# First layer of a retention + two-MLP kernel: seven half products for eight in groups 1 to 3, and everything behind the retention put in order by a list scheduler in the source

## The chip, the cores and the metric

The kernel runs on one core of one Trainium2 chip. The metric is device time of one execution in microseconds (us), as the median of three runs. Engines are named as the profile names them: PE is TensorE (its weight loads are PEld), DVE is VectorE, ACT is ScalarE, POOL is GpSimd, SP is the engine that issues most DMAs.

## What is computed

The reference has three parts, one behind the other: a retention (a decayed running sum of outer products of k and v, read with q) over 2 batches, 8 heads, 768 positions and 64 channels; a first layer pair with a softplus; and a second, gated layer pair behind a norm.

```python
for t in range(S):
    state = gamma[None, :, None, None] * state + np.einsum('bhd,bhe->bhde', k[:, :, t], v[:, :, t])
    y[:, :, t] = scale * np.einsum('bhd,bhde->bhe', q[:, :, t], state)
x = y.transpose(0, 2, 1, 3).reshape(1536, 512)
h = x @ w_in                                   # 512 -> 2048
x = (np.maximum(h, 0.0) + np.log1p(np.exp(-np.abs(h)))) @ w_out      # 2048 -> 512
xn = x / np.sqrt(np.mean(x * x, axis=-1, keepdims=True) + 1e-06) * rms_g
g = xn @ w_gate                                # 512 -> 1536
out = (g * (1.0 / (1.0 + np.exp(-g))) * (xn @ w_val)) @ w_out2       # 1536 -> 512
```

The weights arrive as 64-bit floats and are turned into 32-bit floats on the chip.

## The kernel before

Tokens (1536) lie along the free dimension in three blocks of 512: block 0, block 1 and block 2, which the code calls `LONE`. Channels lie on the 128 partitions. A product of float32 precision is made of three matmuls (`TERMS`): every operand is kept as a rounded high part and the remainder, its low part, and high by high, high by low and low by high are summed in one PSUM bank. The unit of PE work is a matmul of 128 x 128 weights by 128 x 512 tokens.

**Weights.** Each of the 68 weight tiles is loaded as 64-bit words (`st_...`), and its float32 value is put together by `convert`: two ACT passes (`c`, `a`), a shift and a bit operation on DVE (`w`), an integer add on POOL (`c<-w,c`, L206), a DVE pass (`a<-a,c`, L275), the high part on ACT (L224) and the low part (`rounded`, L221) on POOL, or on DVE for w_gate and w_val. Twelve buffers hold finished weights.

**First layer.** w_in has 16 tiles of 128 output channels, in 4 groups of 4. `l1(b, f)` makes the 12 matmuls (`h`) of one tile for one block; the softplus behind it is three ACT passes and one DVE pass that reads PSUM, then a split into high (ACT) and low (DVE). `l2(b, gr, m)` makes 12 matmuls of the product with w_out for a group. The two alternate, `l1` of one block with `l2` of the block before it. The sum over groups of blocks 0 and 1 is kept in SBUF by DVE adds (L601), that of block 2 in PSUM.

**Second layer.** Blocks 0 and 1 and pairs of weight tiles already go through class `Seven`: with x split into two blocks and two halves of the channels, and the weights likewise, seven half products of 6 matmuls each (`p1` to `p7`, banks Q, R, W) take the place of eight. They need sums of weight tiles (`S`, on POOL, L244), sums of token tiles (`T1` to `T4`), three copies out of bank Q (`c1`, `c6`, `c7`, by ACT) that must be done before the next product is added into Q, and adds of the results on DVE. Block 2 goes the plain way (`l3`). `l4` makes the product with w_out2 and adds over pairs.

**Order.** Program order on each engine is the order in which the source emits instructions. Before, that is written by hand: `piece` emits one PE step, then conversions, delayed work from `later(us, do)` against a hand-advanced `clock`, and one step of the chains that do the norm (`mean`, `along`, `scaled`) and the T sums. PE takes its instructions in that order and waits where an operand isn't ready.

Of the kernel before, what the change touches and what calls it, by code (L numbers as in the profile page):

```python
# [20 lines left out]
G1 = 4  # L21
TINY = 1.125 * 2.0 ** -15


@with_exitstack
def retention_softplus_swiglu(ctx: ExitStack, tc: tile.TileContext, q, k, v, w_in, w_out,
# [34 lines left out]
    oldest, kept = list(range(8)), []  # L61
# [5 lines left out]

    def lend():
        oldest.extend(kept)
        kept.clear()  # L70
# [22 lines left out]
    dec = const.tile([P, 2, CPB, H], F32)  # L93
# [21 lines left out]
    causal = const.tile([P, P], F32)  # L115
# [3 lines left out]
    state = [const.tile([P, NP, D], F32, name=f"state{i}") for i in range(2)]  # L119
    faded = const.tile([P, NP, D], F32, name="faded")  # L120
# [18 lines left out]
    st_free, lent = [f"st{i}" for i in range(STAGE)], []  # L139
    lending = []  # L140
# [19 lines left out]
    clock, due, raw, reserved, busy_s = [0.0], [], {}, [0], []  # L160
    raw_used, raw_at, spare = [0] * 3, {}, []

    def later(us, do):
        due.append((clock[0] + us, do))

    def run(all=False):
        for one in list(due):
            if one in due and (all or one[0] <= clock[0]):
                due.remove(one)
                one[1]()  # L170

# [3 lines left out]
    def convert(parts=False):  # L175
# [5 lines left out]
        gated = nm in ("w_gate", "w_val")  # L181
        if len(free) - reserved[0] < 1 or raw_used[spins.get("a", 0)]:
            return False
# [3 lines left out]
        raw_at[key] = spins.get("a", 0)  # L187
# [22 lines left out]
        raw[key] = a  # L210
        if gated and f % 2:
            sums, sa = [], []
            hold = 0 if key == ("w_val", 1) else 2
            reserved[0] += hold

        def used(n):
            for one in (f - 1, f):
                raw_used[raw_at[nm, one]] += n

# [11 lines left out]
        def combine():  # L231
            if busy_s:
                later(1.36, combine)
                return
            busy_s.append(key)
            a0, a1 = raw[nm, f - 1], a
            sa.extend(row(f"s{n}", "s") for n in range(2))
            s1, s2 = (halves(sa[0], p) for p in range(2))
            s3, s4 = (halves(sa[1], p) for p in range(2))
            for out, x0, x1, op in ((s1, halves(a1, 0), halves(a1, 1), ALU.add),  # L240
                                    (s2, s1, halves(a0, 0), ALU.subtract),
                                    (s3, halves(a0, 0), halves(a1, 0), ALU.subtract),
                                    (s4, halves(a0, 1), s2, ALU.subtract)):
                nc.gpsimd.tensor_tensor(out=out, in0=x0, in1=x1, op=op)  # L244
            used(-1)

            def parts():
                places = free if hold else spare
                if len(places) < 2 or clock[0] - freed.get(places[1], 0.0) < 2.7:
                    later(1.36, parts)  # L250
                    return
                reserved[0] -= hold
                for n in range(2):
                    slot["S", nm, f // 2, n] = places.pop(0)
                    sums.append(rows(slot["S", nm, f // 2, n], f"ws_s{n}"))
                    ws["S", nm, f // 2, n] = sums[n]
                    high(sums[n], sa[n])

                def rest():
                    for n, out in enumerate(sums):  # L260
                        rounded(out, sa[n])
                        ready.add(("S", nm, f // 2, n))
                    busy_s.clear()
                later(1.4, rest)
            later(4.0, parts)

        def whole():
            for out, src in ((ws[nm, f - 1], raw[nm, f - 1]), (t, a)):
                rounded(out, src, nc.vector)
            ready.add((nm, f - 1))  # L270
            ready.add(key)
            used(-1)

        def finish():
            nc.vector.scalar_tensor_tensor(out=a, in0=a, scalar=TINY, in1=c.bitcast(F32),  # L275
                                           op0=ALU.is_ge, op1=ALU.mult)
            if not gated:
                if nm == "w_out2":
                    later(2.6, last)
                else:  # L280
                    deferred.append(last)
            else:
                later(2.6, high)
                if f % 2:
                    later(1.3, combine)
                    later(4.0, whole)

        if gated and f % 2:
            used(2)
        ws[key] = t  # L290
        left[key] = 2 if gated else NB
        pos["conv"] += 1

        def done():
            (lent if lending else st_free).append(tag)
            lending[:] = []
# [7 lines left out]
        if nm in ("w_in", "w_out"):  # L304
            deferred.append(finish)
        else:
            later(5.4, finish)
        return True

    def need(key):  # L310
        while key not in ready:
            if due:
                run(True)
            elif deferred:
                flush()
            else:
                assert convert(), key
# [6 lines left out]
    freed = {}  # L324

    def release(tag):
        freed[tag] = clock[0]
        free.append(tag)
# [170 lines left out]
    g_t, acc, tags = {}, {}, {}  # L499
    bg = []  # L500
    chains = []
# [14 lines left out]
    def split_later(key, t):  # L516
        def go():
            n = places.pop(key, None)
            if n is None:
                n = places["next"]  # L520
                places["next"] = (n + 1) % 8
            g = rows(f"g{n}", "g")
            split(g[:, 0], g[:, 1], t)
            g_t[key] = g
        deferred.append(go)
# [26 lines left out]
    def kept_row(b, m, src):  # L552
        tags[b, m] = spin("s2_", 10)
        acc[b, m] = row(tags[b, m], "x2")
        if m % 2 and b == 0:
            nc.vector.tensor_copy(acc[b, m], src)
        else:
            nc.scalar.activation(out=acc[b, m], in_=src, func=AF.Copy)

    def l2_by(b, f):  # L560
        for m in range(KC):
            if f == 0:
                acc[b, m] = bank("l2", kept)
            w = weight("w_out", f, m == KC - 1)
            for n, (i, j) in enumerate(TERMS):
                nc.tensor.matmul(acc[b, m], lhsT=w[:, i, m * P:(m + 1) * P], rhs=g_t[b, f][:, j, :],  # L566
                                 start=(n == 0 and f == 0), stop=(n == 2 and f == G1 - 1))
        g_t.pop((b, f))

        def after():  # L570
            if f == G1 - 1:
                for m in range(KC):
                    kept_row(b, m, acc[b, m])
                lend()
        return after

    def l2(b, gr, m):
        fs = range(gr * G1, (gr + 1) * G1)
        keep = b == NB - 1
        if keep:  # L580
            if gr == 0:
                acc[b, m] = bank("l2", kept)
            p = acc[b, m]
        else:
            p = bank("l2")
        for f in fs:
            w = weight("w_out", f, m == KC - 1)
            for n, (i, j) in enumerate(TERMS):
                nc.tensor.matmul(p, lhsT=w[:, i, m * P:(m + 1) * P], rhs=g_t[b, f][:, j, :],  # L589
                                 start=(n == 0 and f == (0 if keep else fs[0])),  # L590
                                 stop=(n == 2 and f == (F1 - 1 if keep else fs[-1])))
        if m == KC - 1:
            for f in fs:
                g_t.pop((b, f))

        def after():
            if not keep:
                if gr == 0:
                    kept_row(b, m, p)
                else:  # L600
                    nc.vector.tensor_tensor(out=acc[b, m], in0=p, in1=acc[b, m], op=ALU.add)  # L601
            if gr == NG1 - 1:
                norm(b, m)
        return after

    root = {}
    root_t = const.tile([P, NB, CB], F32, name="root_t")  # L610
    small = const.tile([P, 2, CB], F32, name="small")
    sqs, rooted = {}, set()

    def norm(b, m):
        if m == 0:
            root[b] = row(("r", "ms", "r")[b], "root")
            sqs[b] = [rows(f"g{2 + n}" if b == LONE else f"x{2 + 2 * b + n}", "sq", F32) for n in range(2)]
            if b == LONE:
                channels(("n", b), b)
        sq, r = sqs[b], root[b]  # L620

        def high():
            if b == LONE:
                nc.scalar.activation(out=x["n", b][0][m // 2][:, m % 2], in_=acc[b, m], func=AF.Copy, scale=rg[:, m:m + 1])
# [610 lines left out]
```

## Time and profile before

| what | value |
|---|---|
| timed runs | 605.24, 605.32, 605.75 us, median 605.32 us |
| profiled execution | span 603.5 us from its first to its last instruction; no other time is recorded of it |
| PE busy | 596.8 us, 99% of the span |
| DVE, ACT, POOL busy | 452.9, 353.7, 278.0 us (75%, 59%, 46%) |
| chain that ended last | 94% PE |
| instructions | PE 3232, DVE 655, ACT 613, POOL 228 |

The span is what the trace shows; the timed runs lie 1.8 us above it. Busy PE isn't PE at its best, since the ends of pipelined matmuls are modelled; distances between starts tell more than durations.

### The profile page before, as it was taken

To read this page: it belongs to the slowest core of one execution; us is meant where nothing else is said; L and a number is where in the kernel's file an instruction comes from. 1 tells how busy PE (TensorE), PEld (TensorE's weight loads), DVE (VectorE), ACT (ScalarE), POOL (GpSimd) and SP (SyncE) were. 2 spreads that over 40 slices of the span, in tenths; PEclk is the share of its full clock that TensorE was granted. 3 is DMA by queue.
4 is the path that set the end of the run, shared out by engine and by line. 5 is a ranking of instruction groups with operands and counts; after the bars stand their busy time and mean duration, and the time that the engine had idled before them with its cause. 6 is when DMAs were issued, how large, how long until landed. Compare 5 with 4: busy or idle time off the path is not lost.

```text
span 603.5 us, 8624 instructions
## 1 busy us (share of the span) xinstructions
PE 596.8 (99%) x3232; PEld 494.7 (82%) x3232; DVE 452.9 (75%) x655; ACT 353.7 (59%) x613; POOL 278.0 (46%) x228
## 2 busy tenths in 40 slices
PE   8999999999999999999999999999999999999997
PEld 7888888888888888878878888888888888888886
DVE  5788777577777875258788988699799699799545
ACT  3456678787778775287575667653563563554320
POOL 3544344554445442224021277485386387287111
PEclk9999999999999999999999999999999999999999
DMA  9999133233333331121000112322222221320014
GB/s 199 229 222 218 48 106 102 78 99 106 104 81 99 99 105 36 35 64 42 1 2 0 36 35 71 104 71 70 71 71 55 85 71 36 105 70 2 1 53 156
DMA packets 65562, 48.84 MB, mean 81 GB/s; under 512 B 39792, under 2 KB 60528, under 8 KB 65520
## 3 DMA queue, kind: packets, MB, share of 16 engines
q1 hardware_dynamic: 64320, 47.90, 28.3%
q8 instruction: 25, 0.41, 0.3%
q10 hardware_dynamic: 1200, 0.39, 0.3%
q14 instruction: 17, 0.14, 0.1%
HBM read 45.14 MB, written 3.15 MB: 80 GB/s over the span
## 4 chain that ended last, share of the span: by engine, by line
PE 94%; SPq 2%; DVE 1%; DMA 1%; ACT 1%; issue 0%; DVEq 0%
PE h L509 22%; PE l L589 20%; PE l L916 16%; PE Q L806 10%; PE h_w_val L509 5%; PE h_w_gate L509 5%; PE R L806 5%; PE y L469 2%; PE W L806 2%; PE l L566 2%; PE sc L417 2%; SPq L84 1%; PE pt L398 1%; DMA st_w_in<-in_moe_w_in_dram 1%; PE u L436 1%; DVE g L784 0%
## 5 line engine op out<-in xcount | busy, mean ns | idle before, releaser
L206 POOL TENSOR_TENSOR c<-w,c 128x512 uint32<-128x512 uint32 x68 | 90.9, 1337 | 122.4 <-DVE w L202 91.5
L509 PE MATMUL h<-x,ws_w_in 128*128 128x512 f32 x576 | 137.5, 390 | 0.0
L509 PEld LDWEIGHTS h<-x,ws_w_in 128*128 128x128 f32 x576 | 107.7, 188 | 23.1 <-issue 0.7
L589 PE MATMUL l<-g,ws_w_out 128*128 128x512 f32 x528 | 125.4, 390 | 0.0
L589 PEld LDWEIGHTS l<-g,ws_w_out 128*128 128x128 f32 x528 | 98.7, 188 | 20.9 <-DVE g L125 0.6
L916 PE MATMUL l<-ws_w_out,g 128*128 128x512 f32 x432 | 108.2, 389 | 0.0
L916 PEld LDWEIGHTS l<-ws_w_out,g 128*128 128x128 f32 x432 | 81.0, 188 | 17.1 <-DVE g L784 0.3
L547 DVE SCALAR_TENSOR_TENSOR t<-h,t 128x512 f32<-128x512 f32 x48 | 33.1, 690 | 61.1 <-ACT t L540 61.1
L221 POOL TENSOR_TENSOR ws_w_out<-a,ws_w_out 128x512 fp32r<-128x512 f32 x28 | 39.6, 1414 | 57.0 <-ACT ws_w_out L224 57.0
L812 ACT ACTIVATE p<-Q 128x512 f32<-128x512 f32 x36 | 21.4, 596 | 59.1 <-PE Q L806 59.1
L275 DVE SCALAR_TENSOR_TENSOR a<-a,c 128x512 f32<-128x512 f32 x68 | 50.3, 739 | 7.0 <-POOL c L206 7.0
L124 ACT ACTIVATE g<-t 128x512 fp32r<-128x512 f32 x48 | 30.2, 629 | 34.0 <-DVE t L547 34.0
L221 POOL TENSOR_TENSOR ws_s<-s,ws_s 128x512 fp32r<-128x512 f32 x24 | 37.9, 1597 | 25.9 <-ACT ws_s L224 25.9
L535 ACT ACTIVATE t<-h 128x512 f32<-128x512 f32 x48 | 28.6, 596 | 33.2 <-PE h L509 33.1
L784 DVE TENSOR_TENSOR g<-t,g 128x512 fp32r<-128x512 f32 x36 | 36.7, 1043 | 13.3 <-ACT g L783 13.3
L827 POOL TENSOR_TENSOR t<-t,e 128x512 f32<-128x512 f32 x18 | 26.6, 1477 | 34.6 <-DVE e L823 23.2
L125 DVE TENSOR_TENSOR g<-t,g 128x512 fp32r<-128x512 f32 x48 | 33.9, 707 | 8.9 <-ACT g L124 6.0
L946 DVE TENSOR_TENSOR o<-l,o 128x512 f32<-128x512 f32 x39 | 26.6, 684 | 18.0 <-PE l L916 17.9
L806 PE MATMUL Q<-T,ws_s 128*128 128x512 f32 x144 | 36.5, 391 | 0.1
L221 POOL TENSOR_TENSOR ws_w_in<-a,ws_w_in 128x512 fp32r<-128x512 f32 x16 | 22.4, 1397 | 29.3 <-ACT ws_w_in L224 27.9
L202 DVE SCALAR_TENSOR_TENSOR w<-st_w_out,w 128x512 uint32<-128x512 uint32 x28 | 34.0, 1215 | 1.0
L509 PE MATMUL h_w_val<-x,ws_w_val 128*128 128x512 f32 x144 | 34.7, 390 | 0.0
(132 smaller groups left out, 1035.5 us busy)
## 6 DMA issues: line engine op xcount, KB each, us to landing
st_w_out<-in_moe_w_out_dram SPq DMA_DIRECT2D x28, 512.0 KB, 3.4
st_w_in<-in_moe_w_in_dram SPq DMA_DIRECT2D x16, 512.0 KB, 3.8
st_w_gate<-in_moe_w_gate_dram SPq DMA_DIRECT2D x12, 512.0 KB, 3.6
st_w_val<-in_moe_w_val_dram SPq DMA_DIRECT2D x12, 512.0 KB, 3.5
v<-in_v_dram SPq DMA_DIRECT2D x12, 256.0 KB, 4.9
q<-in_q_dram SPq DMA_DIRECT2D x23, 128.0 KB, 4.8
k<-in_k_dram SPq DMA_DIRECT2D x23, 128.0 KB, 3.9
out_dram<-o SPq DMA_DIRECT2D x11, 256.0 KB, 2.0
```

Of the source, the lines that this page charges most:

```text
L124: nc.scalar.activation(out=hi, in_=src, func=AF.Copy)
L125: eng.tensor_tensor(out=lo, in0=src, in1=hi.bitcast(F32), op=ALU.subtract)
L202: nc.vector.scalar_tensor_tensor(out=w, in0=hi32, scalar=0xC0000000, in1=w, op0=ALU.bitwise_and, op1=ALU.bitwise_or)
L206: nc.gpsimd.tensor_tensor(out=c, in0=w, in1=c, op=ALU.add)
L221: eng.tensor_tensor(out=out[:, 1], in0=src, in1=out[:, 0].bitcast(F32), op=ALU.subtract)
L275: nc.vector.scalar_tensor_tensor(out=a, in0=a, scalar=TINY, in1=c.bitcast(F32), op0=ALU.is_ge, op1=ALU.mult)
L509: nc.tensor.matmul(h, lhsT=w[:, i, kk * P:(kk + 1) * P], rhs=src[j][kk // 2][:, kk % 2, :], start=(n == 0), stop=(n == 3 * KC - 1))
L547: nc.vector.scalar_tensor_tensor(out=t, in0=h, scalar=0.0, in1=t, op0=ALU.max, op1=ALU.add)
L589: nc.tensor.matmul(p, lhsT=w[:, i, m * P:(m + 1) * P], rhs=g_t[b, f][:, j, :], start=(n == 0 and f == (0 if keep else fs[0])), stop=(n == ...
L784: nc.vector.tensor_tensor(out=g[:, 1], in0=t, in1=g[:, 0].bitcast(F32), op=ALU.subtract)
L806: nc.tensor.matmul(ps, lhsT=halves(w[:, i], p)[:, kk * P:(kk + 1) * P], rhs=t[j][:, kk, :], start=start and n == 0, stop=n == 5, skip_grou ...
L916: nc.tensor.matmul(ps4, lhsT=g_t[b, f][:, j, m * P:(m + 1) * P], rhs=w[:, i, :], start=n == 0 and (i, j) == TERMS[0], stop=n == 1 and (i, ...
```

## The change

In groups 1 to 3 the first layer of blocks 0 and 1 goes through seven half products too: class `First` is a `Seven` whose results go into the softplus. That needs `forms()` (T1 to T4 from the x of blocks 0 and 1, with their splits) and the sums `S` for the six pairs of w_in tiles of groups 1 to 3. Group 0 and block 2 stay as they were. Behind the retention all work is described as tasks with their reads, writes and buffers, and `Plan.run` emits them by list scheduling from a table of durations written in the source: each engine takes the task that can start first, PE may choose among the next 6 steps of the written order (`WINDOW`), several operations may go to DVE or POOL (`engs` of "V", "G"), copies out of PSUM to ACT or DVE, and buffers come from common pools. Nothing at run time follows that table: it sets program order alone. The retention's own instructions stay in their order; its state, decay, mask and faded tiles move into buffers that are used again later. Weight conversions from the sixth on belong to the scheduler (`EARLY`).

```diff
+    def forms():
+        raw = {}
+        for nm, b, e in (("T1", 1, 0), ("T3", 1, 1), ("T2", 0, 0), ("T4", 0, 1)):
+            raw[nm] = [r2(nm) for _ in range(2)]
+            for n, out in enumerate(raw[nm]):
+                h, l = X[b][0][e], X[b][1][e]
+                add(("V", "G"), (V_2, G_2), lambda en, out=out, h=h, l=l, n=n: two_in(en, out.tile, h.tile[:, n].bitcast(F32),
+                                                                                 l.tile[:, n].bitcast(F32), ALU.add),
+                    reads=[(h, n), (l, n)], writes=[out], opens=[out], soft=True)
+        for n in range(2):
+            less(raw["T3"][n], raw["T3"][n], raw["T1"][n])
+            less(raw["T1"][n], raw["T1"][n], raw["T2"][n])
+            less(raw["T2"][n], raw["T2"][n], raw["T3"][n], ALU.add)
+            less(raw["T4"][n], raw["T4"][n], raw["T2"][n])
+        for nm in ("T1", "T2", "T3", "T4"):
+            parts(nm, raw[nm])
...
+    class First(Seven):
+
+        def out(self, b, n, src, other):
+            key = b, 2 * self.p + n
+            if other is None:
+                soft(key, src)
+            elif (b, n) == (1, 1):
+                self.summed(other, src, other)
+                soft(key, other)
+            else:
+                self.summed(src, src, other)
+                soft(key, src)
...
+    for gr in range(MIX, NG1):
+        A, B = First("w_in", 2 * gr), First("w_in", 2 * gr + 1)
+        if gr == MIX:
+            fill = l2s(LONE, gr - 1)
+            seven(A, "1 2 5 6 F 7 F 4 3", fill)
+            seven(B, "1 2 5 6 F 7 F 4 3", fill)
+        else:
+            seven(A, "1 2 F 5 F 6 F 7 F 4 3", l2s(1, gr - 1))
+            seven(B, "1 2 F 5 F 6 F 7 F 4 3", l2s(LONE, gr - 1))
+        mix("12121212", l1s(LONE, gr), l2s(0, gr))
+    mix("1111", l2s(1, NG1 - 1))
+    mean(0)
+    mix("1", l2s(LONE, NG1 - 1)[:1])
+    along(0)
+    scaled(0)
+    mix("1", l2s(LONE, NG1 - 1)[1:2])
+    mean(1)
+    mix("1", l2s(LONE, NG1 - 1)[2:3])
+    along(1)
+    scaled(1)
+    mix("1", l2s(LONE, NG1 - 1)[3:])
...
+            if e == "V" and t.soft:
+                st = max(st, busy["G"])
+            if e == "G":
+                st = max(st, busy["V"], busy["G"] + 0.02)
+                if t.engs != "G" and t.late < st + self.spare:
+                    return None
+            return st
```

In numbers of emitted instructions: DVE 655 before and 775 now, POOL 228 and 204, ACT with its three DMA issues 616 and 638; PE has 36 matmuls of 128 x 512 fewer.

What PE does at the start of group 1, before: `h` is a plain tile of block 0, `l2` the product of block 2 and group 0.

```order
L509 MATMUL h_1418<-x0_183,ws_w_in_1235 128x512 x2
L509 MATMUL h_1418<-x0_184,ws_w_in_1235 128x512 x2
L509 MATMUL h_1418<-x0_185,ws_w_in_1235 128x512 x2
L509 MATMUL h_1418<-x0_186,ws_w_in_1235 128x512 x2
L509 MATMUL h_1418<-x0_183,ws_w_in_1235 128x512 x2
L509 MATMUL h_1418<-x0_184,ws_w_in_1235 128x512 x2
L589 MATMUL l2_1445<-g_1212,ws_w_out_933 128x512 x3
```

And the same place of PE now: Q, W and R are banks of the first `First`, T1 and T2 token sums, ws_s0 a sum of weight tiles.

```order
L932 MATMUL Q_1436<-x0_178,ws_w_in_1303 128x512 x2
L932 MATMUL Q_1436<-x0_180,ws_w_in_1303 128x512 x2
L932 MATMUL Q_1436<-x0_178,ws_w_in_1303 128x512 x2
L932 MATMUL W_1449<-x0_179,ws_w_in_1303 128x512 x2
L932 MATMUL W_1449<-x0_181,ws_w_in_1303 128x512 x2
L932 MATMUL W_1449<-x0_179,ws_w_in_1303 128x512 x2
L932 MATMUL R_1463<-T1_1324,ws_s0_1419 128x512 x2
L932 MATMUL R_1463<-T1_1355,ws_s0_1419 128x512 x2
L932 MATMUL R_1463<-T1_1324,ws_s0_1419 128x512 x2
L932 MATMUL Q_1436<-T2_1329,ws_s0_1419 128x512 x2
```

Half products of 6 matmuls stand where a tile of 12 stood, and the third of them reads T1 and the low part of ws_s0, which DVE makes in the stretch just before.

The second place is PE between the layers, now: `ms` is the mean of block 1's squares, `root` the spreading of its result over the partitions, with the Newton steps of DVE between the two.

```order
L1178 MATMUL root_3200<-ident_85,root_t_1069 128x128 x4
L932 MATMUL l2_1623<-g_2931,ws_w_out_2750 128x512 x3
L932 MATMUL l2_1623<-g_2958,ws_w_out_2765 128x512 x3
L932 MATMUL l2_1623<-g_3019,ws_w_out_2768 128x512 x3
L932 MATMUL l2_1623<-g_3059,ws_w_out_2784 128x512 x3
L1155 MATMUL ms_3232<-ones_83,sq_3171 128x1 x4
L932 MATMUL l2_1669<-g_2931,ws_w_out_2750 128x512 x3
L932 MATMUL l2_1669<-g_2958,ws_w_out_2765 128x512 x3
L932 MATMUL l2_1669<-g_3019,ws_w_out_2768 128x512 x3
L932 MATMUL l2_1669<-g_3059,ws_w_out_2784 128x512 x3
L1178 MATMUL root_3275<-ident_85,root_t_1069 128x128 x4
L932 MATMUL Q_3286<-B11_3228,ws_w_gate_2952 128x512 x2
```

Before, 24 matmuls of `p1` and `p2` stood between `ms` and `root` of block 1, and all 48 of block 2's `l2` behind that `root`; now 12 of those 48 stand between the two, the other 36 ahead of them, and nothing of `l2` is left behind `root`.

The third place is DVE ahead of the first `l4` (product with w_out2, tiles 0 and 1), now: `T4` is the last token sum of the second layer, `w`, `a` and `ws_w_out2` are steps of the conversion of w_out2's tiles 0 and 1.

```order
L828 TENSOR_TENSOR T4_3535<-x2_1294,T4_3478 128x512
L880 TENSOR_SCALAR w_3547<-st_w_out21_3083 128x512
L883 SCALAR_TENSOR_TENSOR w_3538<-st_w_out20_2977,w_3538 128x512
L883 SCALAR_TENSOR_TENSOR w_3547<-st_w_out21_3083,w_3547 128x512
L1235 TENSOR_TENSOR t_3463<-h_w_val_3505,t_3463 128x512
L1077 TENSOR_TENSOR t_3565<-R_3429,p6_3474 128x512
L1206 TENSOR_TENSOR t_3559<-Q_3297,t_3559 128x512
L1077 TENSOR_TENSOR p6_3486<-R_3443,p6_3486 128x512
L888 SCALAR_TENSOR_TENSOR a_3372<-a_3372,c_3367 128x512
L888 SCALAR_TENSOR_TENSOR a_3397<-a_3397,c_3370 128x512
L828 TENSOR_TENSOR g_3524<-t_3390,g_3524 128x512
L828 TENSOR_TENSOR ws_w_out2_3590<-a_3372,ws_w_out2_3590 128x512
```

And before, DVE between T4 and the same `l4`:

```order
L694 TENSOR_TENSOR T4_3371<-x2_1272,T4_3370 128x512
L773 TENSOR_TENSOR t_3291<-h_w_val_3374,t_3291 128x512
L275 SCALAR_TENSOR_TENSOR a_3339<-a_3339,c_3338 128x512
L694 TENSOR_TENSOR B22_3390<-x2_1396,B22_3389 128x512
L694 TENSOR_TENSOR B22_3390<-x2_1416,B22_3389 128x512
L819 TENSOR_TENSOR t_3407<-R_3246,p7_3402 128x512
L823 TENSOR_TENSOR e_3424<-R_3258,p7_3415 128x512
L221 TENSOR_TENSOR ws_w_gate_3268<-a_3266,ws_w_gate_3268 128x512
L221 TENSOR_TENSOR ws_w_gate_3341<-a_3339,ws_w_gate_3341 128x512
L773 TENSOR_TENSOR t_3328<-h_w_val_3426,t_3328 128x512
L784 TENSOR_TENSOR g_3454<-t_3291,g_3454 128x512
L784 TENSOR_TENSOR g_3457<-t_3328,g_3457 128x512
```

The two w_out2 tiles were converted more than a hundred DVE rows earlier before; now both conversions run through DVE, POOL, DVE, ACT and DVE between T4 and the first `l4`.

## Rows read from the trace of the kernel before

**Rows 1.** The page: span, and busy time, share, instructions of each engine.

```profile
span 603.5 us, 8624 instructions
PE 596.8 (99%) x3232; PEld 494.7 (82%) x3232; DVE 452.9 (75%) x655; ACT 353.7 (59%) x613; POOL 278.0 (46%) x228
```

**Rows 2.** Waits of PE, whole span: waited for, us in total, times, longest.

```profile
PE root L659 <- DVE t L819: 0.4, 1, 0.4
```

**Rows 3.** Chain in order of time, whole span: start, us, what.

```profile
71.50 2.95 PE h L509 x12
...
120.75 2.72 PE h L509 x12
123.47 2.72 PE l L589 x12
...
373.91 1.36 PE Q L806 x6
```

**Rows 4.** Groups by form, DVE and POOL, 96 to 286 us.

```profile
L202 DVE SCALAR_TENSOR_TENSOR w<-st_w_out,w 128x512 uint32<-128x512 uint32 x14 | 13.6, 971 | 0.5
L601 DVE TENSOR_TENSOR x<-l,x 128x512 f32<-128x512 f32 x20 | 13.6, 684 | 0.0
L202 DVE SCALAR_TENSOR_TENSOR w<-st_w_in,w 128x512 uint32<-128x512 uint32 x11 | 13.5, 1226 | 0.4
L198 DVE TENSOR_SCALAR w<-st_w_out 128x512 uint32<-128x512 uint32 x14 | 10.1, 720 | 0.0
L198 DVE TENSOR_SCALAR w<-st_w_in 128x512 uint32<-128x512 uint32 x11 | 7.0, 639 | 0.0
...
L202 DVE SCALAR_TENSOR_TENSOR w<-st_w_val,w 128x512 uint32<-128x512 uint32 x2 | 1.4, 692 | 0.1
L198 DVE TENSOR_SCALAR w<-st_w_val 128x512 uint32<-128x512 uint32 x2 | 0.8, 420 | 0.0
...
L206 POOL TENSOR_TENSOR c<-w,c 128x512 uint32<-128x512 uint32 x29 | 37.5, 1292 | 50.1 <-DVE w L202 46.9 <-PE l L589 3.1
```

**Rows 5.** Timeline around 121 and 420 us: start, us, what.

```profile
120.75 0.63 ACT L124 ACTIVATE g<-t 128x512 fp32r<-128x512 f32 x1 [0.76 <-DVE t L547]
...
122.06 1.54 POOL L221 TENSOR_TENSOR ws_w_out<-a,ws_w_out 128x512 fp32r<-128x512 f32 x1 [1.92 <-ACT ws_w_out L224]
...
122.48 1.67 DVE L202 SCALAR_TENSOR_TENSOR w<-st_w_out,w 128x512 uint32<-128x512 uint32 x1
...
419.37 0.68 DVE L946 TENSOR_TENSOR o<-l,o 128x512 f32<-128x512 f32 x1
419.97 0.68 DVE L773 TENSOR_TENSOR t<-h_w_val,t 128x512 f32<-128x512 f32 x1
```

**Rows 6.** Busy time in stretches: length, PE, PEld, DVE, ACT, POOL, clock, DMA.

```profile
96.00:286.00 190.00, 190.00 (x839) 156.87 (x838) 127.69 (x179) 136.95 (x231) 82.84 (x65) 1.00 0.26 81
...
313.87:351.79 37.92, 37.52 (x172) 30.98 (x173) 33.90 (x57) 22.73 (x41) 10.79 (x8) 1.00 0.05 15
```

**Rows 7.** Chain between the layers, 264 to 352 us.

```profile
299.32 8.18 PE h L509 x36
...
314.92 10.90 PE l L589 x48
...
333.98 0.79 PE ms L643 x8
334.77 2.89 PE Q L806 x12
337.65 0.44 PE root L659 x4
...
346.28 2.95 PE Q L806 x12
```

**Rows 8.** Timeline: the last subtracts of the retention, and one Newton chain's ends.

```profile
71.98 1.28 DVE L125 TENSOR_TENSOR x<-y,x 128x512 fp32r<-128x512 f32 x2
...
334.81 0.16 DVE L645 TENSOR_SCALAR small<-ms 128x4 f32<-128x4 f32 x1
...
336.98 0.17 DVE L654 SCALAR_TENSOR_TENSOR root_t<-small,root_t 128x4 f32<-128x4 f32 x1
```

More of the change, by code (lines that the diff above doesn't have):

```diff
@@ L229, in last @@
             ready.add(key)
[L231 to L272, printed above, removed]
         def finish():
@@ L276, in finish @@
                                            op0=ALU.is_ge, op1=ALU.mult)
[L277 to L289, printed above, removed]
+            deferred.append(last)
         ws[key] = t
-        left[key] = 2 if gated else NB
+        left[key] = NB
         pos["conv"] += 1
         def done():
-            (lent if lending else st_free).append(tag)
-            lending[:] = []
+            st_free.append(tag)
         if parts:
@@ L550, in l1 @@
         return after
[L552 to L604, printed above, removed]
@@ L954, in piece @@
[L954 to L957 removed]
+    def piece(after):
         todo = take()
[L959 to L961 removed]
         for do in todo:
             do()
[L964 removed]
         flush()
[L966 to L975 removed]
+        convert()
+        after()
@@ L1138, in retention_softplus_swiglu, with loads @@
-    two.extend(f"s2_{n}" for n in range(10) if f"s2_{n}" not in tags.values())
-    two.extend(f"t{n}" for n in range(3))
-    lending.append(True)
-    half = 1.36
+    first, second = ([lambda b=b, f=f: l1(b, f) for f in range(G1)] for b in range(2))
+    def loads(*what):
+        for one in what:
+            if one:
+                load(*one)
+            else:
+                load_weight()
+    after = first[0]()
+    loads((6, 1), (7, 0), (7, 1), (6, 2))
+    batch(4, after, True)
+    loads((7, 2), None, None, (8, 0), (8, 1), (9, 0), (9, 1))
@@ new lines, in retention_softplus_swiglu @@
+    batch(6, first[1](), True)
+    loads((8, 2), (9, 2), (10, 0), (10, 1), None)
+    convert()
+    after = first[2]()
+    flush()
+    todo = take()
+    after()
+    for do in todo:
+        do()
+    after = second[0]()
+    loads((11, 0), (11, 1), None)
+    batch(8, after, False)
+    loads((10, 2), (11, 2))
+    piece(first[3]())
+    after = second[1]()
+    todo = take()
+    todo[0]()
+    early = take()
+    deferred.extend(todo[1:])
+    load_weight()
+    batch(10, after, False, early)
@@ new lines, in load_task, with do @@
+    def load_task(i):
+        nm, f = order[i]
+        if i in staged:
+            return mine(ST, "st", *staged[i], 1.5)
+        st = Buf(ST, f"st_{nm}{f}")
+        src = srcs[nm]
+        def do(eng):
+            if nm in ("w_out", "w_out2"):
+                nc.sync.dma_start(out=st.tile, in_=src[f * P:(f + 1) * P])
+            else:
+                nc.sync.dma_start(out=st.tile.rearrange("p (k f) two -> p k f two", k=KC),
+                                  in_=src[:, f * P:(f + 1) * P].rearrange("(k p) f two -> p k f two", p=P))
+        add("S", 1.35, do, writes=[st], opens=[st])
+        return st
@@ new lines, in retention_softplus_swiglu, with weight_of, product, do @@
+    made = [pos["conv"]]
+    def weight_of(nm, f):
+        while (nm, f) not in W:
+            weight_task(made[0])
+            made[0] += 1
+        return W[nm, f]
+    X = {b: [[mine(R4, f"x{b}", x[b][j][e], f"x{4 * b + 2 * j + e}") for e in range(2)] for j in range(2)] for b in range(NB)}
+    G = {key: mine(R4, "g", g_t[key], g_at[key]) for key in g_t}
+    acc = {}
+    XB = {}
+    def product(bank, opens, jobs, reads, starts, stops):
+        n = len(jobs)
+        def do(eng):
+            for k, (lhsT, rhs) in enumerate(jobs):
+                nc.tensor.matmul(bank.tile, lhsT=lhsT(), rhs=rhs(), start=starts and k == 0, stop=stops and k == n - 1,
+                                 skip_group_check=True)
+        return add("P", n * MM, do, reads=reads, writes=[bank], opens=[bank] if opens else [], rest=(n - 1) * MM + 0.39)
@@ new lines, in part_lo, with parts, less @@
+    def part_lo(nm, n, src):
+        b, h = XB[nm][1], XB[nm][0]
+        add(("V", "G"), (V_2, G_2), lambda e: two_in(e, b.tile[:, n], src.tile, h.tile[:, n].bitcast(F32), ALU.subtract),
+            reads=[src, (h, n)], writes=[(b, n)], opens=[b] if n == 0 else [], soft=True)
+    def parts(nm, srcs_):
+        for n, src in enumerate(srcs_):
+            part_hi(nm, n, src)
+        for n, src in enumerate(srcs_):
+            part_lo(nm, n, src)
+    def less(out, x0, x1, op=ALU.subtract):
+        add(("V", "G"), (V_2, G_2), lambda e: two_in(e, out.tile, x0.tile, x1.tile, op), reads=[x0, x1], writes=[out], soft=True)
```

1036 lines of the change are left out of this document (587 added, 449 removed).

## Prediction

> **What bounds the kernel now.** I read the page first: PE is busy for 596.8 of 603.5 us, no other engine above 75% [rows 1]. Busy time of a pipelined engine can hide waiting, so I went on to the chain in order of time: behind the retention, which ends its last outputs at 71.50, PE steps follow each other without a hole, 12 matmuls in 2.72 us and 6 in 1.36 us [rows 3]. That is 0.2267 us for each matmul, at a granted clock of 1.00 [rows 6]. Then the waits: the only one of PE's behind the retention that is listed is 0.4 us for one `root` [rows 2]. So the time behind the retention is the number of matmuls times 0.2267 us, and a matmul less is worth that, as long as DVE, ACT and POOL keep PE fed from new orders. All costs below are therefore of two kinds: matmuls, and time in which PE waits.
>
> **The change, part by part.**
>
> *Matmuls.* Three groups of 4 tiles, 2 blocks and 12 matmuls make 288; six `First` of 7 x 6 make 252. 36 x 0.2267 = **8.16 us** less. Nothing else of 512 columns is added to or taken from PE, so the change does do what it says: no chance is set aside for the opposite.
>
> *Work that moves to DVE.* 120 instructions more, 24 fewer on POOL, 22 more on ACT. At 0.60 us from start to start for a 128 x 512 operation [rows 5] DVE goes from 452.9 [rows 1] to about 525 us of some 598, 88%. Over the whole it still fits; what it costs is decided where PE needs its results soonest. I take two such stretches.
>
> *Stretch 1, retention to the first T1 product.* DVE gets free at 71.98 + 1.28, or 73.2 [rows 8]. PE must have the low part of ws_s0 for the fifth matmul of the third half product: 180 + 4 matmuls behind 71.50, at 113.2. That leaves 40.0 us. In DVE's order 51 instructions stand in it (five shifts, four of half width, 42 of full width): 42 x 0.60 + 9 x 0.42 [rows 4, 5] = 29.0 us, the half widths priced like the shifts, and 10 of POOL's at 1.29 [rows 4], 12.9 us. What POOL costs DVE I take from the trace: a bit operation that began inside a POOL operation took 1.67 us and ended with it [rows 5], where an undisturbed one takes 0.692 [rows 4]. Between 96 and 286 us the bit operations and shifts took 14 x 0.279 + 11 x 0.534 + 14 x 0.300 + 11 x 0.219 = 16.4 us over the undisturbed durations [rows 4], for 82.84 us of POOL [rows 6]: a share of 0.20. So 29.0 + 2.6 = 31.6 us of 40.0: no stall. If every POOL operation held DVE up it would be 41.9, 1.9 us late. Bounds 0 and 1.9; I take 0.5, near the low end, for the chains (DVE, POOL, DVE, ACT, DVE) that each weight goes through.
>
> *Block 1's mean and root.* In the one undisturbed case of before, `root` starts 3.67 us behind the start of `ms` (333.98 to 337.65) [rows 7], 2.34 of them the Newton steps on DVE (334.81 to 336.98 + 0.17) [rows 8]. Now 0.79 + 2.72 = 3.51 us of PE stand there. The stall is 0.16 at least; two operations of 0.60 ahead on DVE's queue make it 1.4. I take 0.2. In return the old place is given back: there PE went from 299.32 to 314.92, 15.6 us, for 36 + 24 matmuls, one `ms` and one `root`, which are 13.60 + 0.79 + 0.44 = 14.83 [rows 7]: **-0.75** (bounds -0.75 and 0).
>
> *Stretch 2, block 1's root to the first `l4`.* This is the tightest. Before, block 2's 48 `l2` matmuls stood behind that `root`, and the w_out2 tiles of the first `l4` were long converted; now neither holds. Between `root` and the sixth matmul of `l4`, which reads the last low part, PE has 137 matmuls, `ms`, and two `root`: 31.06 + 0.79 + 0.88 = 32.7 us, and 0.3 more, an estimate, from the end of the Newton steps to `root` (336.98 + 0.17 to 337.65 [rows 7, 8], half a us at most). DVE has 62 instructions: 12 Newton steps 2.34, two shifts 0.84, 48 others at 0.60 28.8, together 32.0 us. POOL has 10, nine of full and one of half width, 9 x 1.29 + 0.74, about 12.4. With the share of 0.20 DVE needs 34.5 of 33.0 us: 1.5 us late. From the other side: behind T4's last subtract, which PE reads 20 matmuls (4.5 us) before, the last w_out2 tile still needs one shift, 12 operations of 0.60 on DVE with its turns on POOL and ACT (1.29 and 0.63) inside: 7.6 us, so 3.1 us late if T4 is just in time. I take the middle, **2.3 us**. The bounds are 0 (DVE ahead) and 32.0 + 12.4 - 33.0 = 11.4 (every POOL operation holds DVE up).
>
> The Trainium skill, page "SBUF — State Buffer", section "Who interferes with whom", says that a DVE instruction with two SBUF inputs and a GpSimd instruction that reads SBUF exclude each other for a whole instruction, and that one with a single SBUF input doesn't contend. The trace agrees in both directions: the bit operation's 1.67 us, and adds that read PSUM at 684 ns whatever POOL does. By the rule alone, with every POOL operation of stretch 2 in DVE's way, the sum below would end at 608.7 us; by the rows' share it ends at 599.6.
>
> *Copies out of Q.* Eighteen new ones, each to be done before Q is added to again. Of 36 before, two show a lengthened Q step, 0.17 and 0.23 us [rows 7]. At that rate 0.2 us; bounds 0 and 18 x 0.23 = 4.1. ACT, which does most of them, was busy 137 of 190 us there [rows 6], 47 us of a group's 65.3 (288 matmuls by 0.2267); six copies and four high parts of S, at about 0.6 us, make it 53 of 62.6 us, 85%, so the rate may be higher.
>
> *At no cost.* The retention's instructions keep their order and their waits, the tiles it shares now are only taken over later, and loads keep the same count and order but for one or two neighbours; PE's queue is what covers them, and a load that came late would show as a wait for DMA on DVE or ACT.
>
> **Sum.** -8.16 + 0.5 + 0.2 + 2.3 + 0.2 - 0.75 = -5.7 us. On the span: 603.5 - 5.7 = 597.8; the timed runs lie 1.8 us above the span, so 605.32 - 5.7 = **599.6 us**. All low bounds together give -8.75: 596.6.
>
> **The rivals.**
>
> *All of it is kept.* DVE runs ahead in both stretches, and the new copies hide. For it: over the whole DVE has 12% to spare, and it may go ahead as far as buffers allow. Against it: 32.0 us of work for 33.0 us in stretch 2, with POOL's on top. 605.32 - 8.16 - 0.75 + 0.2 to 1.0, about 597.
>
> *Every new Seven waits.* Copies, adds and softplus steps of `First` queue behind conversions, since ACT and DVE are both above 80% there now; each of 18 copies costs 0.23 us instead of one in eighteen, and T sums of the first group come 1.9 us late. For it: ACT had 137 of 190 us already [rows 6]. Against it: a wait of PE lets the others catch up, so it doesn't add up for long. 599.6 + 3.9 + 1.4 = 604.9, no measurable change.
>
> *DVE and POOL exclude each other fully in stretch 2* (the rule above). Slower from the point at which 73% of POOL's 12.4 us fall on DVE there: then the stall is 8.0 instead of 2.3 us and the sum is zero. At 100%: 599.6 - 2.3 + 11.4 = 608.7. For it: both engines are full at this place, so a collision is likelier than the 0.20 of an engine that was 67% busy [rows 6]. Against it: before, DVE was busy 33.90 of 37.92 us in the same part of the work with POOL at 10.79 [rows 6], and PE went through with less than half a us lost.
>
> **How the numbers follow.** 0.2% (1.2 us) is about what a measurement of this kernel can tell from no change: 604.1 to 606.5. Chances: forecast, 598 to 603, 0.52; all kept 0.22; every Seven waits 0.14, half of it below 604.1; full exclusion 0.12. Faster 0.52 + 0.22 + 0.07 = 0.81, same 0.07, slower 0.12. The range goes from all low bounds, 596.5, to 605.0, which leaves out the slower rival, half of the waiting one's upper part and a little below.
>
> **What would show it.** PE's steps of 6 and 12 matmuls still at 1.36 and 2.72 us, and 36 fewer. No wait of PE on T1 or ws_s0 near 113 us. `root` of block 1 within 0.5 us of the `l2` ahead of it. One wait of 1.5 to 3 us at the first `l4`, for a low part of w_out2 from DVE. Q steps of `First` lengthened by at most 0.2 us in a few places. DVE's bit operations under 1.2 us in the mean. Wrong would be: waits spread over groups 1 to 3, a wait at the first `l4` above 5 us, or a retention that ends later than 71.5 us.

## The result

The changed kernel takes 611.81 us (median of 4 runs, 608.78 to 612.19), the kernel before 605.31 (four runs too): slower, by a ratio of 1.009 (95% interval 1.0065 to 1.0114). The forecast was 599.6.

The page of the changed kernel, span and busy time (the line of [rows 1]):

```profile
span 610.1 us, 8653 instructions
PE 593.9 (97%) x3196; PEld 491.0 (80%) x3196; DVE 504.5 (83%) x775; ACT 359.3 (59%) x635; POOL 263.8 (43%) x204
```

PE has its 36 matmuls less and lost more than their time in waits. PE's waits, over the whole span (what is waited for, us in total, times, longest), where [rows 2] had one of 0.4 us behind the retention:

```profile
PE root L1178 <- DVE root_t L1169: 3.4, 1, 3.4
PE l L932 <- ACT ws_w_out L832: 3.3, 1, 3.3
PE l L932 <- DVE x L1006: 2.2, 1, 2.2
...
PE l L932 <- DVE ws_w_out L828: 0.7, 1, 0.7
PE y L579 <- issue: 0.5, 1, 0.5
```

The `l` of the second row is the first `l4`, that of the third an `l2` at 168.52, that of the fourth an `l2` near 84. The chain in order of time (start, us, what) shows two more things:

```profile
113.25 1.36 PE W L932 x6
114.61 1.36 PE R L932 x6
115.97 1.36 PE Q L932 x6
...
319.53 4.54 PE Q L932 x12
...
356.43 1.92 PE l L932 x5
358.36 11.46 PE l L932 x43
```

At 113 us, where the first product with T1 stands, PE goes through at full pace. But the 12 matmuls behind `root` take 4.54 us where 12 took 2.72 [rows 3], and the first 48 of `l4` take 13.38 for 10.88. The granted clock says why (stretch, its length, PE, PEld, DVE, ACT, POOL busy, clock, DMA):

```profile
300.00:320.00 20.00, 16.63 (x85) 13.58 (x84) 17.82 (x39) 10.79 (x19) 11.30 (x10) 1.00 0.09 27
320.00:340.00 20.00, 19.93 (x86) 16.01 (x86) 17.89 (x36) 13.16 (x23) 6.83 (x4) 0.91 0.00 1
340.00:357.00 17.00, 13.70 (x59) 10.79 (x59) 15.29 (x24) 11.73 (x21) 10.41 (x7) 1.00 0.19 62
357.00:370.00 13.00, 12.99 (x48) 9.83 (x48) 11.62 (x19) 7.46 (x13) 7.51 (x4) 0.87 0.33 123
```

Behind each of the two long waits the clock stands at the lower of its two levels (1.2 and 2.4 GHz) for a while: 0.09 x 20 = 1.8 us and 0.13 x 13 = 1.7 us are lost.

Why DVE is late with block 1's `root`: the timeline between the two norms, DVE and POOL.

```profile
310.49 3.10 DVE L1185 SCALAR_TENSOR_TENSOR x<-x,rg,root 128x512 f32<-128x512 f32 x3
311.29 1.75 POOL L828 TENSOR_TENSOR sq<-sq 128x512 f32<-128x512 f32 x1 [5.71 <-DVE x L1185]
312.49 3.02 PE L932 MATMUL l<-g,ws_w_out 128*128 128x512 f32 x12
312.99 1.75 POOL L828 TENSOR_TENSOR ws_s<-s,ws_s 128x512 fp32r<-128x512 f32 x1
313.51 1.78 DVE L828 TENSOR_TENSOR B<-x,B 128x512 fp32r<-128x512 f32 x1
314.70 1.18 POOL L828 TENSOR_TENSOR s<-a 128x256 f32<-128x256 f32 x1
315.21 0.15 DVE L1160 TENSOR_SCALAR small<-ms 128x4 f32<-128x4 f32 x1
315.39 0.51 DVE L1162 TENSOR_SCALAR small<-small 128x4 uint32<-128x4 uint32 x1
315.93 0.65 DVE L1164 TENSOR_SCALAR root_t<-small 128x4 uint32<-128x4 uint32 x1
316.62 0.64 DVE L1167 SCALAR_TENSOR_TENSOR small<-root_t 128x4 f32<-128x4 f32 x1
...
318.88 0.65 PE L1178 MATMUL root<-ident,root_t 128*128 128x128 f32 x4 [3.37 <-DVE root_t L1169]
```

POOL works without a hole, and everything on DVE beside it is stretched: three scaling operations take 3.10 us (2.07 in no_choice below, with POOL still), a subtract 1.78 (0.68), and operations on four numbers per partition up to 0.65 (0.17). In sum 1.03 + 1.10, and 1.29 for the Newton steps (315.21 to 318.83, against 2.33): 3.4 us, as long as the whole wait.

The third place, 157 to 169 us, looks alike. `L956` is the last step of the softplus; where it reads `p`, its input is a sum kept in SBUF, which only `First` has:

```profile
157.00 1.50 POOL L828 TENSOR_TENSOR g<-t,g 128x512 fp32r<-128x512 f32 x1 [1.23 <-ACT g L832]
157.26 3.50 DVE L956 SCALAR_TENSOR_TENSOR t<-p,t 128x512 f32<-128x512 f32 x2
158.46 3.45 POOL L828 TENSOR_TENSOR ws_w_in<-a,ws_w_in 128x512 fp32r<-128x512 f32 x2
160.68 0.68 DVE L1006 TENSOR_TENSOR x<-l,x 128x512 f32<-128x512 f32 x1
...
162.12 1.78 DVE L828 TENSOR_TENSOR g<-t,g 128x512 fp32r<-128x512 f32 x1
...
167.79 0.68 DVE L1006 TENSOR_TENSOR x<-l,x 128x512 f32<-128x512 f32 x1
168.52 1.66 PE L932 MATMUL l<-g,ws_w_out 128*128 128x512 f32 x6 [2.23 <-DVE x L1006]
```

Two `L956` take 3.50 us; two of them take 1.28 in `knobs` below. What stands behind them on DVE is late by that, down to the add at 167.79 that frees the bank PE wants. The short wait near 84 is of the same kind: from 76.0 to 83.6 us, beside POOL, a shift took 1.53 us for 0.42, a bit operation 1.79 for 0.69 and two `a` 3.17 for 1.29, and the low part of w_out that PE wants stands behind them on DVE.

At the first `l4` the picture is another one, of order:

```profile
348.08 0.42 DVE L880 TENSOR_SCALAR w<-st_w_out 128x512 uint32<-128x512 uint32 x1
...
350.12 2.93 POOL L886 TENSOR_TENSOR c<-w,c 128x512 uint32<-128x512 uint32 x2 [3.87 <-DVE w L883]
...
353.78 1.66 DVE L888 SCALAR_TENSOR_TENSOR a<-a,c 128x512 f32<-128x512 f32 x2
...
355.18 0.67 ACT L876 ACTIVATE c<-st_w_val 128x512 uint32<-128x512 uint32 x1 [0.22 <-DMA st_w_val<-in_moe_w_val_dram]
355.76 1.13 ACT L832 ACTIVATE ws_w_out<-a 128x512 fp32r<-128x512 f32 x2
...
356.43 1.92 PE L932 MATMUL l<-ws_w_out,g 128*128 128x512 f32 x5 [3.30 <-ACT ws_w_out L832]
```

The first step of the conversion starts on DVE at 348.08 and the high part is there 8 us later, while PE was free for the product 3.3 us before that.

### The profile page after: what moved, and what is told of

Read it like the earlier page. It is cut to its first block, busy times and chain, and to the rows that moved or that the text cites. A ratio compares the mean times of both kernels' runs of the same rounds, so it can differ in the third digit from the quotient of the medians.

```text
span 610.1 us, 8653 instructions
## 1 busy us (share of the span) xinstructions
PE 593.9 (97%) x3196; PEld 491.0 (80%) x3196; DVE 504.5 (83%) x775; ACT 359.3 (59%) x635; POOL 263.8 (43%) x204
## 4 chain that ended last, share of the span: by engine, by line
PE 87%; DVE 10%; issue 1%; DMA 1%; ACT 1%; DVEq 0%; SPq 0%; ACTq 0%
PE l L932 35%; PE Q L932 15%; PE R L932 7%; PE h L932 6%; PE h_w_gate L932 4%; PE h_w_val L932 4%; PE W L932 3%; PE h L617 3%; PE y L579 2%; PE sc L527 2%; PE pt L508 2%; DVE x L1185 1%; PE u L546 1%; DMA st_w_val<-in_moe_w_val_dram 1%; DVE T L828 1%
## 5 line engine op out<-in xcount | busy, mean ns | idle before, releaser
L932 PE MATMUL h<-x,ws_w_in 128*128 128x512 f32 x216 | 51.2, 390 | 0.0
L828 DVE TENSOR_TENSOR g<-t,g 128x512 fp32r<-128x512 f32 x53 | 43.7, 831 | 5.9 <-ACT g L832 5.6
L932 PEld LDWEIGHTS Q<-T,ws_s 128*128 128x128 f32 x216 | 40.5, 188 | 8.9 <-DVE T L828 0.5
L932 PEld LDWEIGHTS h<-x,ws_w_in 128*128 128x128 f32 x216 | 40.5, 188 | 8.6 <-issue 0.2
L828 POOL TENSOR_TENSOR g<-t,g 128x512 fp32r<-128x512 f32 x25 | 35.9, 1440 | 24.0 <-ACT g L832 23.9
L932 PE MATMUL h_w_gate<-x,ws_w_gate 128*128 128x512 f32 x144 | 34.5, 391 | 0.0
L932 PEld LDWEIGHTS h_w_gate<-x,ws_w_gate 128*128 128x128 f32 x144 | 26.9, 188 | 5.8 <-ACT ws_w_gate L832 0.3
L932 PEld LDWEIGHTS h_w_val<-x,ws_w_val 128*128 128x128 f32 x144 | 27.0, 188 | 5.6
L832 ACT ACTIVATE ws_s<-s 128x512 fp32r<-128x512 f32 x36 | 22.4, 625 | 14.7 <-DVE s L828 9.3
L932 PE MATMUL R<-T,ws_s 128*128 128x512 f32 x108 | 27.2, 389 | 0.0
```

Source lines behind the costliest of these rows:

```text
L828: {"V": nc.vector, "G": nc.gpsimd}[eng].tensor_tensor(out=out, in0=in0, in1=in1, op=op)
L832: nc.scalar.activation(out=out, in_=src, func=AF.Copy)
L932: nc.tensor.matmul(bank.tile, lhsT=lhsT(), rhs=rhs(), start=starts and k == 0, stop=stops and k == n - 1, skip_group_check=True)
```

## The experiments

"Theory 1" and "theory 2" in the expectations are those of each experiment. Runs of one kernel differ by 0.7 to 6.7 us here, in part by how often the clock goes down, so each verdict rests on the trace too.

**The same kernel again**, as a base.

> The changed kernel once more, as the base of the three others. Expected 609 to 612 us, with the same three waits of PE (DVE's add near 166 us, root of block 1, first l4) and one to three stretches of 3.4 us at the lower clock. If the waits stand elsewhere, or the time is under 607 us, the profile shown first was an outlier and the other expectations fall with it.

612.06 us (610.46 to 613.40); waits of 0.8, 2.2, 3.4 and 3.4 us at the same four places, two stretches of lower clock, this time behind the 2.2 (0.72 over 6 us) and the `l4` (0.83 over 10), and none behind `root`. As expected, at the upper end of the range. The first `h` behind the retention starts at 71.53 us here, at 72.40 in the first profile.

**Conversion due earlier** (`weight_of` marks the tasks of w_out2's tiles 0 and 1 with `lead = 10.0`):

```diff
-            t.late = late
+            t.late = late - t.lead
```

> The scheduler is told that the conversion of the first two tiles of w_out2 is due 10 us earlier. Theory 1 (order: DVE and POOL had room, the conversion was only put too late): the 3.3 us wait at the first l4 goes, and with it the stretch of lower clock behind it, 1.7 us; 611.8 - 5.0 = 606.8 us. Theory 2 (DVE with POOL is full between block 1's root and the first l4): the same work moved forward pushes the root or the T sums back by as much, and the time stays at 610 to 613 us.

606.83 us. The row of the first `l4` is gone from PE's waits, the others stand:

```profile
PE root L1183 <- DVE root_t L1174: 3.4, 1, 3.4
PE l L937 <- DVE x L1011: 2.2, 1, 2.2
...
PE l L937 <- DVE ws_w_out L829: 0.8, 1, 0.8
```

Theory 1: this wait was one of order, and no other wait grew. In the profiled run, which took 606.45 us, the clock behind `root` was 0.66 over 10 us, so 3.4 us are lost there; the clock's share of the gain did not show in it.

**Idle time filled** (`filler` writes into the bank that the next product overwrites):

```diff
         def do(e):
+            if b == 1:
+                for _ in range(24):
+                    nc.tensor.matmul(t.tile[:, 0:P], lhsT=ident, rhs=ident, start=True, stop=True)
             for i in range(CB):
...
+        def filler():
+            g = G[b, 0].tile
+            for _ in range(12):
+                nc.tensor.matmul(bank.tile, lhsT=g[:, 0, 0:P], rhs=g[:, 0, :], start=True, stop=True, skip_group_check=True)
```

> 24 matmuls of 128 columns more ahead of block 1's root and 12 of 512 columns more ahead of the first l4, in banks that are written over; results stay the same. Theory 1 (PE's idle of over 3 us brings the clock down to 1.2 GHz behind it, 3.4 us long, at a price of 1.7 us each time): granted clock 1.00 throughout, both waits shorter in the trace but ending where they ended, 611.8 - 3.4 = 608.4 us. Theory 2 (the clock falls for another reason, or the waits end later because of the added work): 611 to 614 us.

612.29 us, with the clock at 1.00 from 300 to 370 us: theory 1 on the clock, theory 2 on the time, because the 24 products made 48 matmuls that took 5.5 us in all, at a wait of 3.4. That run tells nothing about the price, so it was repeated with 12:

> fill_idle again with half the fill ahead of the root (12 products of 128 columns in two passes each, 24 records of 0.11 us, 2.7 us), since 5.4 us outlasted the wait of 3.4. Theory 1 (idle PE of over 3 us brings the clock down, 1.7 us each): no stretch of lower clock behind the root or the first l4, both waits end where they ended, 612 - 2 x 1.7 = 608.6 us, or 610.3 where the wait near 166 us still brings the clock down. Theory 2: 612 us or more with the clock at 1.00.

609.80 us (608.47 to 611.80). PE's timeline around `root`:

```profile
317.75 2.84 PE L1181 MATMUL root<-ident 128*128 128x128 f32 x24
321.32 0.65 PE L1183 MATMUL root<-ident,root_t 128*128 128x128 f32 x4 [0.73 <-DVE root_t L1171]
321.72 1.82 PE L934 MATMUL Q<-B,ws_w_gate 128*128 128x512 f32 x6
```

`root` still comes 3.57 us after its first chance, and the matmuls behind run at full pace. The clock went down once, behind the 2.2 us near 166, which wasn't filled. The median is 2.3 us lower, between the 1.7 of one stretch and the 3.4 of two, but the four runs overlap with those of `again`: the price of 1.7 us stands on the rows of the clock, and this time only agrees with it. That idle PE brings the clock down stands on the traces: over all profiled runs here the lower clock followed eight of the nine waits of 3.0 to 3.6 us, and it came at neither of the two filled places, in fill_idle and in fill_short.

**The scheduler alone**, all of the first layer plain:

```diff
-MIX = 1
+MIX = 4
```

(with the then useless `forms()` and a second call of the last `l2` taken out.)

> The list scheduler alone: all four groups of the first layer as plain eight products, 36 matmuls more than the changed kernel. Theory 1 (the waits between the layers come from the scheduler's order there): root and first l4 still wait, about 3 us each with their clock stretches, the waits near 84 and 166 us go: 611.8 + 8.2 - 3.3 = 616.7 us, range 613 to 619. Theory 2 (the 120 DVE instructions that First adds are what costs): without them PE never waits, as before, 605 to 606 us.

617.64 us: theory 1 on the total. The waits are partly others (`root` 0.5, `l` on a low part of g 2.7 in two places, first `l4` 2.5); near 84 and 166 there is none. PE has 3232 instructions, as many as before [rows 1], so what the scheduler writes, order and POOL's share together, costs 12.3 us without `First`, and the seven products then give 5.6 back (617.64 to 612.06): it isn't the work that `First` adds that makes the kernel slow.

**POOL without a choice:**

```diff
-SPARE = 3.0
+SPARE = 1000.0
```

> The changed kernel with SPARE at 1000: the 105 operations that the scheduler gave to POOL of its own choice go to DVE, POOL keeps its 63 integer adds. Theory 1 (a POOL operation holds a two-input DVE operation up for its whole time, and the waits near 166 us and at block 1's root come from that): both waits, 2.2 and 3.4 us, shrink to under 1 us, their clock stretches go, the wait at the first l4, which is one of order, stays at 3 to 4.5 us; 612 - 5 - 1.7 = 605 us, range 603 to 607. Theory 2 (DVE lacks time): DVE gets some 55 us of work more, 504 + 55 = 559 us, 92% of the span, PE waits in more places and the time is 614 us or more.

608.44 us: 3.4 more than expected, outside the range. The two waits shrank as theory 1 has it (0.6 us, and none at `root`), and the one near 84 is gone too, but the wait at the first `l4`, 3.0 us, came with a clock of 0.77 over 15 us, two stretches' worth (3.4 us lost), and four of 0.4 to 1.2 us came up. The page and the Newton steps say what POOL's help was worth:

```profile
PE 593.7 (98%) x3196; PEld 490.2 (81%) x3196; DVE 513.6 (85%) x881; ACT 359.5 (59%) x634; POOL 128.9 (21%) x99
```

```profile
L1162 DVE TENSOR_SCALAR small<-small x3: 170/170/170, 300.2 to 319.5; 128x4 uint32<-128x4 uint32 x3
L1164 DVE TENSOR_SCALAR root_t<-small x3: 170/170/170, 300.4 to 319.7; 128x4 uint32<-128x4 uint32 x3
```

(name, times, then shortest, median and longest in ns.) In the changed kernel the same two are 507/794/1081 and 649/930/1210. DVE took over 105 operations, 135 us of POOL's time, and was busy 9 us longer. In this order the `ms` of block 1 also stands earlier, so `root` is not cleared by POOL's silence alone.

**Both edits:**

> Both edits: SPARE at 1000, and the first two w_out2 tiles due 10 us earlier. Theory 1: what is left is waits of under 1.5 us each between the layers, none long enough to bring the clock down; 605 - 3.5 - 1.7 = 600 us, range 598 to 602, faster than the kernel before. Theory 2: DVE is full between the layers, what is put forward holds something else up, 604 us or more.

601.56 us, ratio 0.9939 (0.9922 to 0.9955): theory 1, faster than the kernel before. No wait behind the retention above 1.0 us, clock 0.999.

**Both edits, first layer plain:**

> The same two edits with the first layer as plain eight products: 36 matmuls more than no_choice_due. Theory 1 (without waits the seven products are worth their matmuls): 8.2 us above no_choice_due, 608 us. Theory 2 (the 120 operations that First adds cost PE time even without the choice of POOL): the difference is 4 us or less.

610.41 us, 8.85 above: theory 1. Without long waits the seven products are worth about their 36 matmuls (8.16); runs of each kernel spread over 2.4 to 2.6 us, and the profiled spans differ by 8.1, so the 0.7 us beyond 8.16 can't be told from noise. This kernel has as many matmuls as the one before and still takes 5.2 us more (605.21 to 610.41): that part of the scheduler's cost stays without POOL's choice. In its profiled run, 6.7 us above the kernel before, 2.4 us of wait stand in the retention and 3.5 in six waits of up to 1.0 behind it.

**POOL kept off one stretch** (on top of the earlier due time):

```diff
-                if t.engs != "G" and t.late < st + self.spare:
+                if t.engs != "G" and (t.late < st + self.spare or 225 < st < 245):
```

> due_earlier with the scheduler's choice of POOL forbidden in one stretch alone, 225 to 245 us of its own time, about 300 to 320 us of the trace: around the two norms. Theory 1 (the root's wait is made by POOL's operations beside DVE's Newton steps and the scaling ahead of them): Newton's twelve steps take 2.3 us as before and not 3.6, the wait at block 1's root falls from 3.4 to about 0.5 us and brings no lower clock; what is kept off POOL comes on DVE's queue, so 1 to 3 us of waits come up before the first l4; 606.8 - 2.9 - 1.7 + 2 = 604 us, range 602.5 to 606. Theory 2 (DVE's own order keeps Newton back): root still waits 2.5 us or more, 606 us or more.

611.71 us: outside the range. `root` waits 0.5 us as theory 1 says, but not as it says why: block 0's Newton steps took 2.3 us, those of block 1 still 5.5 beside POOL's delayed `ws_s`, and were covered because two `l2` now stood behind `ms`. What was kept off came back at other places, and with it the clock (the second row stood in due_earlier already):

```profile
PE l L937 <- DVE g L829: 2.4, 1, 2.4
PE l L937 <- DVE x L1011: 2.2, 1, 2.2
PE R L937 <- DVE t L1082: 1.2, 1, 1.2
```

The mean clock was 0.989, the lowest of the profiled runs; it fell near 166 too, where nothing was changed. This run says that forbidding POOL in this stretch alone doesn't help; it doesn't prove the cause at `root`.

**One word for the scheduler:** in `soft` it is told that the last softplus step is in POOL's way when its sum lies in SBUF.

```diff
-op1=ALU.add), reads=[src, t], writes=[t])
+op1=ALU.add), reads=[src, t], writes=[t], soft=src.pool is R2)
```

> The changed kernel with one word added: the softplus operation of First that reads a sum kept in SBUF is marked as one that POOL gets in the way of, as the others are. Theory 1 (that the scheduler did not know this is what makes PE wait near 166 us): that operation at 0.69 us and not 1.79, the wait of 2.2 us there under 1 us, the root and the first l4 as they were; 612 - 1.5 = 610.5 us, 609 to 611.5. Theory 2 (DVE is simply full there): the wait stays at 2 us or more.

609.69 us, in the range. One of the two operations was clear (0.69), one still ran into POOL (1.78); the wait fell from 2.2 to 0.5, theory 1:

```profile
PE root L1178 <- DVE root_t L1169: 3.4, 1, 3.4
PE l L932 <- ACT ws_w_out L832: 3.3, 1, 3.3
...
PE l L932 <- DVE x L1006: 0.5, 1, 0.5
```

**The scheduler's numbers, without and with POOL's choice.** `knobs` is no_choice_due with `WINDOW = 12`, `SLACK = 10.0` and 8 us of lead; `knobs_pool` is the same with `SPARE = 3.0`.

> SPARE at 1000, WINDOW 12, SLACK 10, and the first two w_out2 tiles due 8 us earlier. Theory 1: the scheduler's table holds on the chip once POOL does only what DVE cannot, so that the rest of the waits of no_choice_due (4 us in all behind the retention) can be ordered away as well: no wait of PE above 0.5 us behind the retention, clock 1.00, 601.5 - 4 = 597.5 us, range 596 to 600. Theory 2: DVE at 85% cannot be ordered better, waits of 3 us or more in sum come back elsewhere, 600 to 604 us.

> The same WINDOW, SLACK and due time, but SPARE left at 3, so that the scheduler gives POOL operations of its choice. Theory 1 (POOL and DVE exclude each other, and where POOL starts off its planned time the plan falls): several waits of 1 to 5 us, lower clock behind the longest, 606 to 613 us. Theory 2 (the other three numbers made knobs fast, POOL's share matters little): within 2 us of knobs.

599.29 us (ratio 0.9899, 0.9875 to 0.9924) and 607.15: theory 1 for knobs_pool, and 7.9 us between them, for one number. That number sets who does the work and, through the scheduler, also the order on every engine; the runs don't part the two. `knobs` is the fastest of all kernels here, 1.8 us slower than expected but within its range. Against theory 1 it still has one wait of PE behind the retention:

```profile
PE l L937 <- DVE t L961: 2.1, 1, 2.1
```

Ahead of it DVE operations ran into POOL's remaining integer adds, a shift of 1.52 us for 0.41 at 162.29 and two `g` of 2.37 for 1.28 at 167.94: 2.2 us in sum. `knobs_pool` waits 3.6 us at a `root` and 1.9 near 142, each with its stretch of lower clock. Ahead of that `root` DVE lost 1.04 us in three scaling operations, 0.55 in a subtract and 1.34 in the Newton steps, with POOL busy beside them: 2.9 of the 3.6, by the same sum as in the changed kernel.

## Why the prediction was wrong

The forecast sum was -5.7 us; the profiled spans differ by +6.6.

| step of the sum | forecast | measured |
|---|---|---|
| 36 matmuls | -8.16 | -8.16; 8.85 between the two kernels without long waits |
| stretch 1, to the T1 product | +0.5 | no wait at T1; 0.7 near 84, within the stretch, and 2.2 near 166, which no step looked at |
| block 1's mean and root | +0.2 | +3.4 |
| stretch 2, to the first `l4` | +2.3 | +3.3 |
| copies out of Q | +0.2 | 0 |
| old place of the root | -0.75 | -0.4, its listed wait, which is gone |
| lower clock | not in the sum | 2 x 1.7 |
| retention | 0 | +1.0 (first `h` behind it at 72.40 for 71.43), not by the change |

The matmuls stand, and of stretch 2 the place of the wait and its late conversion. The measured column comes to +5.4. The other 1.2 us show in the starts of PE's matmuls: from start to start the four waits are 0.7 us longer than their rows say, and the first matmuls of `l4` lose 0.5 more, waiting for low parts of w_out2. The two lengthened Q steps of [rows 7] were no waits for copies, as I had read them: in each only the first matmul takes longer, by 0.1 us, as others right behind an `ms` or a `root` do.

The step that failed first is the price of POOL beside DVE. Over the whole DVE was less busy than forecast (504.5 us for 525); the price was wrong where both engines were full. "A share of 0.20" was a mean over 190 us in which POOL was busy 83 [rows 6]. It also counted shifts and bit operations alone, and took the bit operation of [rows 5] to end with POOL's operation, where it ended 0.55 us behind it (124.15 to 123.60). Between the norms DVE lost 3.4 us to 6.1 us of POOL (1.75 + 1.75 + 1.18 + 2 x 0.72): 0.56. So "I take 0.2" for the root was too small by 3.2 us: the two operations that I had priced at 0.60 ahead of Newton were there, but took 1.77 and 1.78, and the Newton steps themselves 3.62 for 2.34 [rows 8]. "DVE and POOL exclude each other fully" was the right mechanism among the rivals, with 0.12 of the chance, but I had put it at the first `l4`, where order made the wait: it stays at 3.0 us without POOL's choice (no_choice) and goes with the earlier due time. The Trainium skill, page "SBUF — State Buffer", section "Who interferes with whom", calls it an exclusive lock for the whole instruction, for two SBUF inputs and for single-input `tensor_scalar` in a two-port mode, and says that the order of issue decides who blocks: the trace agrees (1.78 for 0.68; a shift of 1.52 for 0.41). My prediction left the second case out, though the shifts of [rows 4], with one SBUF input, took 720 and 639 ns for 420, and it weighed the rule against an average, where it should have been applied operation by operation. What is shown for `root` is this sum, in two kernels, and that the wait is absent with POOL still; no run silenced POOL there with all else in place.

The second failure: the forecast had no price for a wait beyond its length. Rows of before never showed the lower clock between the retention and the last matmuls, where PE never waited longer than 0.4 us. Each of the two long waits cost half as much again.

The third: I took "two such stretches" and left out the rest. The `l2` of 168.52 waits for a bank, through DVE's queue, behind an operation that only `First` has, and the `l2` near 84 behind conversions held up by POOL.

"A retention that ends later than 71.5 us" came true, but not by the change: PE stood 0.5 us in `y` near 57 us, with nothing for the profile to name, and `again`, the same kernel, has no such wait. It is 1.6 us in no_choice_due, 2.4 in plain_no_choice and missing in `knobs`, all with the same retention. Its cause stays open.

## What to carry to other kernels

Work given to a second engine that locks the first one out was no help here: 105 operations moved back to DVE cost it 9 us of busy time, and with the order made anew for it the same choice took 7.9 us off the kernel. A list scheduler in the source needs every operation that collides marked, and the mark alone doesn't keep them apart on the chip (one of two still collided); leave to the locking engine what nothing else can do. Price PE's waits with what follows them, and where a change moves a whole order, look at each of PE's steps rather than at the two tightest.

## What the runs showed of the hardware that was not expected

DVE operations on 4 numbers per partition, with one SBUF input, took up to 1.21 us beside POOL and 0.17 without it. The lower clock took 1.7 or 3.4 us at a place, and not always the same one: behind the 2.2 us near 166 it came in `again`, fill_short and quiet_root and not in the changed kernel's profiled run, due_earlier and fill_idle; behind the 3.4 us at `root` it came in the changed kernel and not in `again`; in knobs_pool it came behind 1.9 us, in `knobs` not behind 2.1.
